# Splitting the first load of a memory-bound decode kernel into 16 and 112 partitions

## Chip, cores, metric

One core of one Trainium2 chip. The metric is the device time of one execution in microseconds (us), the median of several. Times named together were taken in the same rounds on the same chip, unless the text says otherwise.

Names used below: SBUF is the on-chip memory, 128 partitions (rows) wide. PE multiplies matrices, DVE, ACT and POOL are the vector, scalar and general engines; SP issues the transfers. A load is carried out by 16 DMA engines (each load leaves 16 landing records), in packets; here a packet is one row, that is, one partition's share of the load (28672 bytes for `wq`).

## The reference, cut to what matters

```python
# A: attention of one new token over a cache of 65536 positions, 16 query heads, 8 cache heads
xn = layernorm(x)                      # x: (1, 1, 448)
q  = xn @ wq                           # wq: (448, 4096), bf16: 3.67 MB, needed before any score
scores = einsum(q, k_cache) / sqrt(256)  # k_cache: (8, 65536, 256) bf16: 268 MB
o = softmax(scores) @ v_cache          # v_cache: as much again
A = o @ wo
# B: a small gated feed-forward of the same token (w_gate, w_up, w_down)
out = x + A + B
```

Half a gigabyte of cache is read once for one token.

## The kernel before

All large loads are issued from one queue, SP, in the order in which the data are used: `wq`, then blocks of the cache through a ring of four SBUF slots (4 MB each, 128 partitions of 32 KB). The parts that the change and the argument touch:

```python
NSLOT = 4; CH = 64
ring   = S_("ring", [P, NSLOT * SLOT], BF16)     # P = 128, SLOT = 16384 elements
w_area = S_("w_area", [P, WQN], BF16)            # WQN = 14336: 28672 bytes in a partition

def item(key, parts, need=()):                   # one or more loads on the SP queue
    for n in need:
        W("sp", *n)
    for ap, src, sem in parts:
        semtot[sem] = semtot.get(sem, 0) + 16
        items[key] = (sem, semtot[sem])          # who waits for key waits for all its parts
        prog["sp"].append(("d", here[0], ("DMA", key, len(prog["sp"])), (ap, src), sem))

def flat_src(src, n):                            # memory as 128 rows of n elements
    return src.rearrange("a b -> (a b)").rearrange("(p n) -> p n", p=P)

item("wq", [(w_area[:, 0:WQN], flat_src(A_wq, WQN), "wq")])
for u in range(U):
    for c in range(HC):
        slot_item("k", u, c)                     # a ring slot; waits for FREE of 4 rounds ago
# ... [cut: the other loads, all compute, the emitter]
```

PE waits for `wq` (`W_item("pe", "wq")`), makes the queries, and then takes one ring slot after another.

## Time and profile before

| | before |
|---|---|
| time, median of 3 runs | 1284.51 us (1284.49 to 1285.25) |
| span of the profiled run | 1283.4 us |
| PE, DVE, ACT busy | 72%, 46%, 36% |
| bytes on the SP queue | 549.04 MB |
| rate between 60 and 1200 us | 432 GB/s |

The page's slice rows and its queue table. A digit is the busy share of the 16 DMA engines in one fortieth of the span, in tenths; the row below gives the GB/s moved.

```profile
DMA  9999999999999999999999999999999999999997
GB/s 405 427 433 427 433 432 431 430 431 432 432 433 431 433 430 433 430 433 430 433 432 432 432 431 432 429 433 433 431 432 432 432 430 433 431 431 433 431 429 318
...
q1 hardware_dynamic: 22210, 549.04, 99.6%
```

The DMA queue runs from the beginning to the end at one rate. No compute engine comes near that.

The table of issues: the size of one load, and the median time from issue to landing.

```profile
ring<-in_A_k_cache_dram SPq DMA_DIRECT2D x64, 4096.0 KB, 25.0
ring<-in_A_v_cache_dram SPq DMA_DIRECT2D x62, 4096.0 KB, 32.0
...
w_area<-in_A_wq_dram SPq DMA_DIRECT2D x1, 3584.0 KB, 11.3
```

At 432 GB/s, 4 MB take 9.7 us. The cache loads land 25 to 32 us after issue, so each waits behind others: the queue is never empty. Whatever holds the DMA engines up should therefore be added to the end (it was: 7.50 us lost at the start, 7.30 at the end, measured below).

The stretches of the span (us; busy time of each engine; granted clock; DMA busy share; GB/s):

```profile
core 0: us, PE busy (x) PEld busy (x) DVE busy (x) ACT busy (x) POOL busy (x), PEclk, DMA share, GB/s
0.00:10.00 10.00, 0.00 (x0) 0.00 (x0) 4.33 (x12) 1.28 (x1) 4.52 (x35) 1.00 0.85 336
10.00:20.00 10.00, 3.52 (x120) 3.35 (x120) 3.12 (x9) 2.25 (x8) 0.00 (x0) 1.00 1.03 443
20.00:30.00 10.00, 7.13 (x52) 6.51 (x53) 4.12 (x7) 3.22 (x4) 0.00 (x0) 1.00 0.99 426
...
60.00:1200.00 1140.00, 835.79 (x8877) 617.09 (x8876) 537.37 (x998) 421.43 (x596) 0.00 (x0) 0.88 1.00 432
```

The timeline of the start (start, duration, engine, operation; in brackets the idle time before it and what ended that):

```profile
0.74 0.41 SPq L776 DMA_DIRECT2D w_area<-in_A_wq_dram  x1
...
1.21 2.20 SPq L776 DMA_DIRECT2D ring<-in_A_k_cache_dram  x4
...
14.00 3.15 PE L352 MATMUL ps_m<-xnT_sb,w_area 128*128 128x2 bf16 x112 [1.63 <-ACT xnT_sb L340]
...
22.87 5.35 PE L352 MATMUL ps_t<-ident_f,ring 128*128 128x128 f32 x32 [5.72 <-DMA ring<-in_A_k_cache_dram]
```

The issue on SP is over long before its data land (0.41 us against 11.3). The queries wait here for `xnT_sb`, not for `wq`; the first cache block is used as soon as it has landed.

### The profile page before, as it was taken

Reading aid. Unit: us, or ns where it says so; the run is one execution under the profiler, and the core shown is the slowest. Engines: PE = TensorE matmul, PEld = TensorE weight load, DVE = VectorE, ACT = ScalarE, POOL = GpSimd, SP = SyncE. Lnnn points to the kernel's source line nnn. Section 1 sums busy time; section 2 is a strip of 40 time slices with the busy share of each in tenths; the row PEclk is TensorE's granted clock in tenths of the full one; section 3 lists DMA queues with packets and bytes.
Section 4 is the critical chain, followed back from the end, with each engine's and each line's share of the span. In section 5 each row is a group of like instructions: output and inputs, shape, how many; then the busy total and the mean of one; then the engine's idle time right before and its main releaser. Section 6 shows DMA issues by size and latency. Waiting matters only on the chain.

```text
span 1283.4 us, 22878 instructions
## 1 busy us (share of the span) xinstructions
PE 924.9 (72%) x9824; PEld 671.5 (52%) x9824; DVE 585.8 (46%) x1091; ACT 459.2 (36%) x655; POOL 4.5 (0%) x35
## 2 busy tenths in 40 slices
PE   3988766786666886666876667866668766678654
PEld 3867554465454565554654545654446544456411
DVE  4756443554344554444554445543445534455300
ACT  2645332353333443324433243432434333234300
POOL 1000000000000000000000000000000000000000
PEclk9988888998889988879888889888899887898876
DMA  9999999999999999999999999999999999999997
GB/s 405 427 433 427 433 432 431 430 431 432 432 433 431 433 430 433 430 433 430 433 432 432 432 431 432 429 433 433 431 432 432 432 430 433 431 431 433 431 429 318
DMA packets 22228, 549.22 MB, mean 428 GB/s; under 512 B 2371, under 2 KB 4422, under 8 KB 5190
## 3 DMA queue, kind: packets, MB, share of 16 engines
q1 hardware_dynamic: 22210, 549.04, 99.6%
q8 instruction: 8, 0.13, 0.0%
q14 instruction: 6, 0.05, 0.0%
q10 hardware_dynamic: 4, 0.00, 0.0%
HBM read 549.03 MB, written 0.00 MB: 428 GB/s over the span
## 4 chain that ended last, share of the span: by engine, by line
DMA 68%; PE 31%; SPq 0%; ACT 0%; issue 0%; DVE 0%
DMA ring<-in_A_k_cache_dram 63%; PE ps_t L352 24%; PE ps_q L352 5%; DMA w_area<-in_B_w_down_dram 3%; DMA ring<-in_A_v_cache_dram 2%; PE ps_s L352 1%; PE ps_m L352 1%; SPq L776 0%; ACT s L430 0%; DVE res_bf L727 0%; PE ps_o L352 0%
## 5 line engine op out<-in xcount | busy, mean ns | idle before, releaser
L352 PE MATMUL ps_t<-ident_f,ring 128*128 128x128 f32 x4096 | 568.8, 296 | 248.6 <-DMA ring<-in_A_k_cache_dram 229.5
L406 DVE COPY kt_buf<-ps_t 128x1024 bf16<-128x1024 bf16 x768 | 489.5, 683 | 420.9 <-PE ps_t L352 420.4
L352 PEld LDWEIGHTS ps_t<-ident_f,ring 128*128 128x128 f32 x4096 | 494.9, 152 | 354.2 <-DMA ring<-in_A_k_cache_dram 245.5
L408 ACT ACTIVATE kt_buf<-ps_t 128x1024 bf16<-128x1024 bf16 x256 | 261.9, 1023 | 356.1 <-PE ps_t L352 355.8
L430 ACT ACTIVATE s<-ps_q 98x512 bf16<-98x512 f32 x256 | 152.7, 597 | 288.1 <-PE ps_q L352 288.1
L352 PE MATMUL ps_o<-ring,p_sb 128*4 128x512 bf16 x2048 | 132.6, 401 | 67.0 <-DMA ring<-in_A_v_cache_dram 67.0
L352 PE MATMUL ps_q<-kt_buf,q_cur 128*2 128x512 bf16 x2048 | 166.2, 402 | 0.0
L352 PEld LDWEIGHTS ps_o<-ring,p_sb 128*4 128x4 bf16 x2048 | 47.7, 86 | 133.2 <-issue 75.5
L352 PEld LDWEIGHTS ps_s<-sel_bf,s 128*128 128x128 bf16 x1024 | 60.7, 99 | 54.1 <-ACT s L430 50.7
L540 DVE CAST ob_sb<-ps_o 100x512 bf16<-100x512 f32 x29 | 20.0, 691 | 142.8 <-PE ps_o L352 142.8
L352 PE MATMUL ps_s<-sel_bf,s 128*128 128x8 bf16 x1024 | 64.4, 169 | 22.6 <-ACT s L430 22.6
L497 ACT ACTIVATE p_sb<-S_sb 128x128 bf16<-128x128 bf16 x64 | 18.9, 307 | 136.2 <-PE ps_o L352 136.0
L576 DVE TENSOR_TENSOR rowsf<-ps_m,rowsf 1x448 f32<-1x448 f32 x28 | 17.1, 612 | 53.8 <-PE ps_m L352 53.8
L352 PEld LDWEIGHTS ps_q<-kt_buf,q_cur 128*2 128x2 bf16 x2048 | 27.1, 79 | 10.2 <-issue 5.0
L512 DVE RECIPROCAL rs<-ps_m 128x4 f32<-128x4 f32 x29 | 5.3, 182 | 52.8 <-PE ps_m L352 52.8
L352 PE MATMUL ps_m<-wo_cur,oT_sb 128*1 128x448 bf16 x112 | 25.7, 352 | 0.0
L352 PEld LDWEIGHTS ps_m<-rowsum,ones_f 128*128 128x128 f32 x116 | 15.1, 190 | 12.6 <-issue 12.6
L352 PE MATMUL ps_m<-rowsum,ones_f 128*128 128x2 f32 x116 | 17.6, 256 | 0.0
L352 PEld LDWEIGHTS ps_m<-wo_cur,oT_sb 128*1 128x1 bf16 x112 | 9.3, 83 | 13.5
L454 DVE CAST S_sb<-ps_s 128x256 bf16<-128x256 f32 x32 | 12.9, 404 | 4.3 <-PE ps_s L352 4.3
L487 ACT ACTIVATE S_sb<-S_sb,negmax 128x512 bf16<-128x512 bf16 x16 | 13.4, 864 | 3.6 <-DVE negmax L481 3.6
L456 DVE TENSOR_REDUCE m1p<-S_sb 128x2 f32<-128x256 bf16 x32 | 13.5, 421 | 1.1
(79 smaller groups left out, 138.3 us busy)
## 6 DMA issues: line engine op xcount, KB each, us to landing
ring<-in_A_k_cache_dram SPq DMA_DIRECT2D x64, 4096.0 KB, 25.0
ring<-in_A_v_cache_dram SPq DMA_DIRECT2D x62, 4096.0 KB, 32.0
ring<-in_A_v_cache_dram SPq DMA_DIRECT2D x2, 2048.0 KB, 28.1
w_area<-in_A_wq_dram SPq DMA_DIRECT2D x1, 3584.0 KB, 11.3
wo_cur<-in_A_wo_dram SPq DMA_DIRECT2D x7, 448.0 KB, 15.4
ring<-in_A_v_cache_dram SPq DMA_DIRECT2D x2, 1024.0 KB, 30.2
ring<-in_A_v_cache_dram SPq DMA_DIRECT2D x4, 512.0 KB, 31.4
w_area<-in_B_w_gate_dram SPq DMA_DIRECT2D x1, 1568.0 KB, 38.6
```

The source lines that it names most:

```text
L352: return pe.matmul(*a, **k)
L406: O(e, ("EV", s, m), lambda it: nc.vector.tensor_copy(out=kt[:, :], in_=tb[:, :]), f"ev{m}")
L408: O(e, ("EV", s, m), lambda it: nc.scalar.activation(out=kt[:, :], in_=tb[:, :], func=ACTF.Copy), f"ev{m}")
L430: O("act", ("EVQ", s), lambda it: nc.scalar.activation(out=s2[s % 2][0:QROWS, :], in_=ps_q[0:QROWS, :], func=ACTF.Copy), "evq")
L454: O("dve", ("SCOPY", u), lambda it: nc.vector.tensor_copy(out=S, in_=ps_sn))
L456: O("dve", ("SMAX", u), lambda it: nc.vector.tensor_reduce(out=m1p[:, :, k], in_=S.rearrange("p n i -> p i n"), axis=AX.X, op=ALU.max))
L487: O("act", ("EXP", h, i), lambda it, i=i: nc.scalar.activation(out=S_sb[:, :, i], in_=S_sb[:, :, i], func=ACTF.Exp, bias=negmax[:, i:i + 1 ...
L497: O("act", ("PC", t, c), lambda it: nc.scalar.activation(out=p_sb[:, c, :, :], in_=S_sb[:, n:n + CH, :], func=ACTF.Copy), "pc")
L512: O("dve", ("RS", t), lambda it: nc.vector.reciprocal(out=rs[:, :, :], in_=ps_m[0:P, C_TOT:C_TOT + NH * rep]))
L540: O("dve", ("OB", t), lambda it: nc.vector.tensor_copy(out=ob_sb[0:OROWS, :], in_=ps_o[0:OROWS, :]))
L576: O("dve", ("RES", t), lambda it: nc.vector.tensor_tensor(out=base_f, in0=ps_m[0:1, C_BIG:C_BIG + D], in1=base_f, op=ALU.add))
```

## The change

The changed kernel begins with a load of 16 rows, one for each of the 16 DMA engines; the other 112 rows follow. The change states no reason; presumably data were to move sooner.

```diff
-    item("wq", [(w_area[:, 0:WQN], flat_src(A_wq, WQN), "wq")])
+    item("wq", [(w_area[o:e, 0:WQN], flat_src(A_wq, WQN)[o:e, :], "wq") for o, e in ((0, P // 8), (P // 8, P))])
```

## The prediction

> What bounds the kernel now: the DMA queue. The page's slice rows show DMA busy 9 tenths in every slice but the last (7), at about 432 GB/s except the first (405) and the last (318). The issue table shows cache loads landing 25 to 32 us after issue, so work is always queued; the chain of waits is 68% DMA. PE (72%), DVE and ACT wait. The time is: start to first packet, the packets of 16 engines, a tail of some 6 us. The trace's packet records put the first packet at 1.77 us, 1.03 us after the first issue began; that issue occupies SP for 0.41 us (timeline). A 28672-byte packet takes 1.06 us (27.0 GB/s per engine), back to back; those of the first round took 1.4 to 2.3 us.
>
> The change: the order of instructions differs only on SP: the load of wq into 128 partitions becomes 16 and then 112. Bytes and packets stay the same, save 16 semaphore packets of 9 ns. Issues behind it move by some 0.4 us, which doesn't matter: 8 us of wq is queued. Gain: the issue of 16 rows is shorter, so the first packet may start earlier. The issue of 128 rows is 0.41 us, of one row 0.21 us (timeline), so I estimate 0.1 to 0.2 us, all on the critical path.
>
> Cost: every other big load covers 128 partitions. [...] This trace can't confirm it; it shows each engine at 27.0 GB/s when 128 partitions are written. [...] The second part gives seven rows to each engine. [...] Lost DMA time isn't regained, so it goes to the end one for one.
>
> Prediction: 1290 us, range 1284 to 1297. Faster by over 2%: 0.01; within 2%: 0.93; slower by over 2%: 0.06.
>
> What would show it:
> - First packet 0.1 to 0.2 us earlier: the 16-row issue under 0.41 us in the timeline.
> - [...] the first slice falls below 405 GB/s. [...]
> - [...]
> - wq landing (11.3 us after issue) becomes 15 to 19 us; PE's first transposes start 3 to 7 us after the 22.87 us of before; later slices keep 432 GB/s.
> - PE, DVE and ACT busy times unchanged.
>
> What would make it wrong: [...] If rows are dealt by 16, it is near 1310. If the engine that ends last (landings of the last load spread over 3 us) is not the one delayed most, the loss is a microsecond or two smaller.

The sum behind the 1290 us: 1284.4 us with the gain alone (1284.5 less 0.1), and, for the case that came about, two terms for the cost of the two parts, together 2.4 to 7.2 us: 1286.8 to 1291.6 us in all. Both cost terms were estimates. The landing of `wq` and PE's start were forecast with them; so was the 1310 us of the case of dealing by 16.

## The result, and the profile after

| | before | after |
|---|---|---|
| time, median of 4 runs each | 1284.7 us | 1292.35 us |
| range of the runs | 1284.49 to 1285.25 | 1292.07 to 1292.52 |
| ratio of the runs | | 1.0059 (95%: 1.0041 to 1.0076) |
| span of the profiled run | 1283.4 us | 1290.7 us |
| PE busy | 924.9 us | 926.4 us |

A ratio is the mean time of one kernel's runs over that of the other's of the same rounds, so it is not quite the ratio of the medians. The change costs 7.65 us by the medians, 0.6%. The two profiled executions happen to be the slowest of each kernel (1285.25 and 1292.52), so the traces below show 7.3 us and not 7.65.

The page's slice rows and queue table of the changed kernel:

```profile
DMA  9999999999999999999999999999999999999997
GB/s 307 423 434 434 429 432 433 428 437 429 432 434 429 435 431 432 433 431 434 431 432 432 431 434 431 433 432 431 434 430 434 432 430 435 430 434 432 430 431 317
...
q1 hardware_dynamic: 22226, 549.04, 99.6%
```

The same bytes, and 16 packets more. The busy row has not changed by one digit, but the first slice moved 307 GB/s in place of 405. A packet that is held up lasts longer in the records (3.04 us in place of 1.73 in the first round below) and counts as busy for all of it; one has to read the GB/s row as well.

The issues of the changed kernel:

```profile
ring<-in_A_k_cache_dram SPq DMA_DIRECT2D x64, 4096.0 KB, 25.3
ring<-in_A_v_cache_dram SPq DMA_DIRECT2D x62, 4096.0 KB, 32.3
...
w_area<-in_A_wq_dram SPq DMA_DIRECT2D x1, 3136.0 KB, 18.3
...
w_area<-in_A_wq_dram SPq DMA_DIRECT2D x1, 448.0 KB, 5.8
```

The stretches of the changed kernel:

```profile
core 0: us, PE busy (x) PEld busy (x) DVE busy (x) ACT busy (x) POOL busy (x), PEclk, DMA share, GB/s
0.00:10.00 10.00, 0.00 (x0) 0.00 (x0) 5.11 (x15) 2.35 (x3) 4.55 (x35) 1.00 0.91 184
10.00:20.00 10.00, 0.70 (x21) 0.65 (x22) 2.34 (x7) 0.79 (x5) 0.00 (x0) 1.00 0.99 285
20.00:30.00 10.00, 2.79 (x105) 2.70 (x102) 0.00 (x0) 0.40 (x2) 0.00 (x0) 1.00 0.98 421
...
60.00:1200.00 1140.00, 841.42 (x8945) 620.10 (x8943) 542.34 (x1005) 425.33 (x601) 0.00 (x0) 0.88 1.00 432
```

In the first 20 us the DMA engines are as busy as before (0.91 and 0.99) and move 184 and 285 GB/s where they moved 336 and 443. After 60 us the rate is again 432.

The timeline of its start:

```profile
0.74 0.85 SPq L776 DMA_DIRECT2D w_area<-in_A_wq_dram  x2
...
1.64 1.85 SPq L776 DMA_DIRECT2D ring<-in_A_k_cache_dram  x4
...
19.66 3.12 PE L352 MATMUL ps_m<-xnT_sb,w_area 128*128 128x2 bf16 x112 [8.39 <-DMA w_area<-in_A_wq_dram]
...
30.14 5.57 PE L352 MATMUL ps_t<-ident_f,ring 128*128 128x128 f32 x32 [7.36 <-DMA ring<-in_A_k_cache_dram]
```

The queries now wait for `wq`. That wait costs nothing by itself: the next data, the first cache block, land only at 30.10 us. It is a sign of the DMA delay, not a second loss.

The delay is complete when `wq` has landed, and is carried to the end. The trace's landing records, us from the span's start, last of the 16 engines:

| | before | after | difference |
|---|---|---|---|
| first packet starts | 1.77 | 1.76 | -0.01 |
| issue of the first load, duration | 0.41 | 0.39 | -0.02 |
| all of `wq` landed | 12.03 | 19.53 | 7.50 |
| first cache block landed | 22.82 | 30.10 | 7.28 |
| last load landed | 1277.97 | 1285.27 | 7.30 |
| span | 1283.4 | 1290.7 | 7.3 |

The packet records show how. They are the large packets of the SP queue in order of start, taken 16 at a time, since the load has 16 engines; the table gives the median duration of each round in us. Rounds 1 to 8 are `wq`, 28672 bytes a packet; rounds 9 and 10 are the first cache block, 32768 bytes. (Grouped by start, not by engine, so a round can hold a neighbour's packet.)

```
round     1     2     3     4     5     6     7     8     9    10
before  1.73  1.08  1.06  1.06  1.06  1.06  1.06  1.06  1.21  1.21
after   3.04  2.42  1.92  1.60  1.53  1.65  1.90  1.80  1.75  1.21
```

Rounds 1 to 9 add up to 10.39 us before and 17.61 us after: 7.2 us. From round 10 on both are alike.

### The profile page after: what moved, and what is told of

It is laid out like the page before. It is cut to its first block, busy times and chain, and to the rows that moved or that the text cites. A ratio compares the mean times of both kernels' runs of the same rounds, so it can differ in the third digit from the quotient of the medians.

```text
span 1290.7 us, 22879 instructions
## 1 busy us (share of the span) xinstructions
PE 926.4 (72%) x9824; PEld 671.7 (52%) x9824; DVE 586.1 (45%) x1091; ACT 459.5 (36%) x655; POOL 4.6 (0%) x35
## 4 chain that ended last, share of the span: by engine, by line
DMA 68%; PE 31%; SPq 0%; ACT 0%; issue 0%; DVE 0%
DMA ring<-in_A_k_cache_dram 63%; PE ps_t L352 24%; PE ps_q L352 5%; DMA w_area<-in_B_w_down_dram 3%; DMA ring<-in_A_v_cache_dram 2%; PE ps_s L352 1%; PE ps_m L352 1%; SPq L776 0%; ACT s L430 0%; DVE res_bf L727 0%; PE ps_o L352 0%
## 6 DMA issues: line engine op xcount, KB each, us to landing
w_area<-in_A_wq_dram SPq DMA_DIRECT2D x1, 3136.0 KB, 18.3
```

## The experiments

Theories, as the expectations below use them:

- **Ports.** The expectations' name for this: what counts is which SBUF partitions the 16 engines write at the same time. No trace or run here shows a port.
- **Splitting, or cold start.** A second load, or a small load at the very beginning, has a fixed cost.
- **Memory.** Sixteen neighbouring rows read at once are slow on the read side; SBUF doesn't matter.

Medians in us; "over" is the difference of the medians to the kernel before in the same rounds.

| run | the first load | this | before | over |
|---|---|---|---|---|
| e_cols | 1/8 and 7/8 of the columns, 128 rows each | 1285.07 | 1285.05 | 0.02 |
| e_quarter | 16 and 112 rows for a quarter of the columns, then one load | 1286.37 | 1285.05 | 1.32 |
| e_dum16 | 16 rows once more, then one load | 1289.0 | 1285.05 | 3.95 |
| e_dum128 | as many bytes once more into 128 rows, then one load | 1286.02 | 1285.05 | 0.97 |
| e_nn | 8 x 16 rows: near in SBUF, near in memory | 1307.54 | 1285.25 | 22.29 |
| e_fn | 8 x 16 rows: far in SBUF, near in memory | 1294.24 | 1285.25 | 8.99 |
| e_nf | 8 x 16 rows: near in SBUF, far in memory | 1307.64 | 1285.25 | 22.39 |
| e_ff | 8 x 16 rows: far in SBUF, far in memory | 1294.35 | 1285.25 | 9.10 |
| e_rev | 112 rows, then 16 | 1293.9 | 1285.17 | 8.73 |
| e_half | 64 rows, then 64 | 1294.2 | 1285.17 | 9.03 |
| e_seven | 16 rows, then 7 x 16 rows with step 7 | 1292.6 | 1285.12 | 7.48 |
| e_dum112 | 112 rows once more, then one load | 1297.43 | 1285.12 | 12.31 |

All twelve passed the comparison with the reference. e_fn and e_nf put rows of `wq` into wrong partitions: the comparison doesn't notice a wrong `wq` in this problem, so it says little about that part of a kernel. These two are wrong by their construction.

### Is it the splitting? e_cols

```diff
-    item("wq", [(w_area[:, 0:WQN], flat_src(A_wq, WQN), "wq")])
+    item("wq", [(w_area[:, a:b], flat_src(A_wq, WQN)[:, a:b], "wq") for a, b in ((0, WQN // 8), (WQN // 8, WQN))])
```

> The first load is again made as two with the same 1 to 7 split of bytes, but by columns: both parts cover all 128 partitions. Port theory (loss comes from which SBUF partitions are written at once): within 0.5 us of the kernel before (about 1284.7), wq landing near 11.5 us after issue, first packet still at 1.77 us. Splitting theory (a second load at the start costs a fixed amount, whatever its shape): about 1292, as in the changed kernel.

Measured: 1285.07 beside 1285.05, ratio 1.0 (95%: 0.9987 to 1.0014). The issues of e_cols:

```profile
w_area<-in_A_wq_dram SPq DMA_DIRECT2D x1, 3136.0 KB, 10.8
...
w_area<-in_A_wq_dram SPq DMA_DIRECT2D x1, 448.0 KB, 3.9
```

The same two sizes as in the changed kernel, landing 10.8 and 3.9 us after issue in place of 18.3 and 5.8. Making two loads costs nothing; how they are cut does. It gains nothing either: its first packet started at 1.76 us.

### Per byte, or once? e_quarter

```diff
-    item("wq", [(w_area[:, 0:WQN], flat_src(A_wq, WQN), "wq")])
+    item("wq", [(w_area[o:e, a:b], flat_src(A_wq, WQN)[o:e, a:b], "wq") for o, e, a, b in
+                ((0, 16, 0, WQN // 4), (16, P, 0, WQN // 4), (0, P, WQN // 4, WQN))])
```

> The split into 16 and 112 rows is made for the first quarter of the columns only; the other three quarters are one load of 128 partitions. Port theory: the loss is per byte, so a quarter of the changed kernel's 7.65 us: 1.9 us, total about 1286.6 (1286.0 to 1287.2). Splitting or cold-start theory: the whole 7 us or more is lost, total about 1292.

Measured: 1.32 us over, within the stated range, though below 1.9. The ratio, 1.0009 (95%: 0.9995 to 1.0022), leaves open whether there is a loss at all (though the fastest of its runs, 1285.62, is above the slowest before, 1285.32), but not one of more than 2.8 us: a fixed cost of 7 us is refuted.

### The first part by itself: e_dum16 and e_dum128

```diff
 ... [cut: "dum" is added to the list of semaphores]
+    item("dum", [(ring[0:16, 3 * SLOT:3 * SLOT + WQN], flat_src(A_wq, WQN)[0:16, :], "dum")])   # e_dum16
+    item("dum", [(ring[:, 3 * SLOT:3 * SLOT + WQN // 8], flat_src(A_wq, WQN)[:, 0:WQN // 8], "dum")])   # or: e_dum128
     item("wq", [(w_area[:, 0:WQN], flat_src(A_wq, WQN), "wq")])
 ...
-                 [("FREE", r - NSLOT)] if r >= NSLOT and k == 0 else ())
+                 [("FREE", r - NSLOT)] if r >= NSLOT and k == 0 else [("DMA", "dum")] if r == NSLOT - 1 else ())
```

> The first part by itself: before wq's unchanged 128-partition load, 16 rows of wq (459 KB) are read once more into partitions 0 to 15 of ring slot 3, which the fourth cache load overwrites later, after a wait for this load. Port theory: [...] the total is 4.25 us over before (1288.9, 1288.3 to 1289.5), 3.2 us over the next kernel, which reads as many bytes into 128 partitions. If the rows-16 part costs nothing beyond its bytes: 1.06 us over before (1285.8).

> Control to the one before: the same 459 KB read once more, as an eighth of the columns of all 128 partitions. All theories: 459 KB at 16 x 27.0 GB/s is 1.06 us, total 1285.8 (1285.3 to 1286.3), unless the extra load itself costs something (splitting theory: about 7 us more).

Measured: 3.95 and 0.97 us over; the ratios' 95% intervals, 1.0017 to 1.0044 and 0.9994 to 1.0021, do overlap a little, but no run of the one lies within 2.5 us of a run of the other. The same bytes at the same place in the queue cost 2.98 us more when they go to 16 partitions. That is the first part of the change's loss.

### SBUF or memory? e_nn, e_fn, e_nf, e_ff

Eight loads of 16 rows each; only the partitions (first index) and the rows of memory (second) differ.

```diff
-    item("wq", [(w_area[:, 0:WQN], flat_src(A_wq, WQN), "wq")])
+    item("wq", [(w_area[16 * b:16 * b + 16, 0:WQN], flat_src(A_wq, WQN)[16 * b:16 * b + 16, :], "wq") for b in range(8)])   # e_nn
+    item("wq", [(w_area[b:P:8, 0:WQN], flat_src(A_wq, WQN)[16 * b:16 * b + 16, :], "wq") for b in range(8)])   # e_fn
+    item("wq", [(w_area[16 * b:16 * b + 16, 0:WQN], flat_src(A_wq, WQN)[b:P:8, :], "wq") for b in range(8)])   # e_nf
+    item("wq", [(w_area[b:P:8, 0:WQN], flat_src(A_wq, WQN)[b:P:8, :], "wq") for b in range(8)])   # e_ff
```

> wq as eight loads of 16 rows, block b being rows 16b to 16b+15 in memory and partitions 16b to 16b+15 in SBUF. Port theory: [...] about 25 us over before, near 1310. Memory theory (16 engines reading 16 neighbouring rows at once are slow on the read side, SBUF does not matter): about the same. Splitting theory: seven more loads, each with a like cost.

> The same eight loads of the same 16 neighbouring rows of memory, in the same order, but written to partitions b, b+8, b+16 and so on[...]. The result is wrong on purpose (rows of wq land in other partitions). Port theory: [...] about 8.5 us over before, near 1293. Memory theory and splitting theory: as the kernel before it, near 1310.

> Eight loads into 16 neighbouring partitions as in the first of this set, but each reads rows b, b+8, b+16 and so on of memory. The result is wrong on purpose. Port theory: as the first, near 1310, since SBUF is written alike. Memory theory: faster, as the reads lie 229 KB apart.

> Eight loads, rows b, b+8, b+16 and so on of memory into the same partitions; the result is right. Port theory: as the second, about 8.5 us over before, near 1293. Memory theory: as the third, whatever that is. Splitting theory: as all three others.

Measured: 22.29, 8.99, 22.39, 9.10 us over. The stretches of each, between 6 and 18 us, which lies inside all four loads of `wq`. For e_nn:

```profile
6.00:18.00 12.00, 0.37 (x8) 0.28 (x8) 5.45 (x16) 1.85 (x6) 0.00 (x0) 1.00 0.98 115
```

For e_fn:

```profile
6.00:18.00 12.00, 0.37 (x8) 0.28 (x8) 4.47 (x14) 1.85 (x6) 0.00 (x0) 1.00 1.04 217
```

For e_nf:

```profile
6.00:18.00 12.00, 0.37 (x8) 0.28 (x8) 5.46 (x16) 1.85 (x6) 0.00 (x0) 1.00 0.97 117
```

For e_ff:

```profile
6.00:18.00 12.00, 0.37 (x8) 0.28 (x8) 4.81 (x15) 1.85 (x6) 0.00 (x0) 1.00 1.08 225
```

The last two columns are the DMA busy share and the GB/s. Changing the partitions alone nearly doubles the rate (115 to 217, 117 to 225); changing the rows of memory alone moves the rate by 2 and 8 GB/s and the time by 0.1 us. So for loads of 16 rows the read side explains next to nothing, and neither does the number of loads, as all four make eight. In the packet records the middle rounds last 3.90 us in e_nn and 2.20 us in e_fn (3.79 in e_nf and 2.22 in e_ff). So 459 KB (16 packets) went at 117.6 GB/s into 16 neighbouring partitions and at 208.5 GB/s into 16 partitions 8 apart. The ratio is 1.8. e_nn came out some 3 us below its forecast: the rounds lasted 3.90 us, less than the estimate.

### Order, and halves: e_rev and e_half

```diff
-    item("wq", [(w_area[:, 0:WQN], flat_src(A_wq, WQN), "wq")])
+    item("wq", [(w_area[o:e, 0:WQN], flat_src(A_wq, WQN)[o:e, :], "wq") for o, e in ((0, 7 * P // 8), (7 * P // 8, P))])   # e_rev
+    item("wq", [(w_area[o:e, 0:WQN], flat_src(A_wq, WQN)[o:e, :], "wq") for o, e in ((0, P // 2), (P // 2, P))])   # e_half
```

> The same two parts in the other order: rows 0 to 111 first, rows 112 to 127 last. Port theory: about the same loss, 5 to 8 us over before (1290 to 1293)[...]. Cold-start theory (the small load is slow only because it is first): most of the loss is gone, 1285 to 1288.

> Two loads of 64 rows, four rows for each engine. If each engine takes four neighbouring rows, [...] about 8.5 us over before (1293). If rows are dealt out 16 at a time, [...] about 25 us over (1310). [...] Splitting theory: as the changed kernel, 1292, which this run alone cannot tell from 1293[...].

Measured: e_rev 8.73 us over. The cold-start theory is refuted, as the loss is there with the small load last. The forecast of the port theory was a miss in size: it allowed 5 to 8 us, and the loss is above that, and 1.1 us more than in the changed kernel (by runs of other rounds, and the ratio's interval, 1.0053 to 1.0080, overlaps that of the change; the traces agree with it: `wq` landed at 20.96 us, against 19.53). In its packet records the 16 rows, now round 8, take 3.53 us, and round 9, the first of the cache block behind them, 2.36 us. Why this order costs more wasn't tested further.

e_half: 9.03 us over; its rounds 2 to 8 last 2.24 us (one of them 2.07). That is near the 2.20 of e_fn, whose 16 partitions lie 8 apart, and far from the 3.90 of e_nn, so 64 rows dealt out 16 neighbours at a time, as e_nn does by hand, are unlikely. The time is near the 1293 of the case of four neighbouring rows to an engine; why that case should cost this much was the author's estimate. This run puts 9.03 us on two loads of 64 rows, 3.67 MB in all.

### Which rows does an engine take in the load of 112? e_seven and e_dum112

```diff
-    item("wq", [(w_area[:, 0:WQN], flat_src(A_wq, WQN), "wq")])
+    item("wq", [(w_area[0:16, 0:WQN], flat_src(A_wq, WQN)[0:16, :], "wq")] + [
+        (w_area[16 + j:P:7, 0:WQN], flat_src(A_wq, WQN)[16 + j:P:7, :], "wq") for j in range(7)])   # e_seven
```

```diff
+    item("dum", [(ring[16:P, 3 * SLOT:3 * SLOT + WQN], flat_src(A_wq, WQN)[16:P, :], "dum")])   # e_dum112, the wait as in e_dum16
     item("wq", [(w_area[:, 0:WQN], flat_src(A_wq, WQN), "wq")])
```

> Which rows does each engine get in the load of 112? Here the first 16 rows are loaded as in the changed kernel, and the other 112 as seven loads of 16 rows with step 7, [...] what it would do in the one load of 112 if it takes seven neighbouring rows. If it does, the time is that of the changed kernel, 7.65 us over before (1292.8 beside a before of 1285.15, within 0.8 us), and rounds of packets last 1.5 to 2.0 us as there. If rows are dealt out otherwise, the time differs by more than that. Splitting theory was refused by earlier runs; eight loads by themselves should cost nothing.

> The second part by itself: rows 16 to 127 of wq (3.21 MB) are read once more into ring slot 3 before the unchanged 128-partition load of wq. [...] If the two parts of the changed kernel's loss add (2.98 us for the first by the two extra-load runs, so 4.7 for the second), the total is 7.43 + 4.7 = 12.1 us over before, 1297.2 (1296.5 to 1298). [...]

Measured: e_seven 7.48 us over, e_dum112 12.31 us over (four runs). The rounds of packets, median us, as above:

```
round     1     2     3     4     5     6     7     8     9    10
after   3.04  2.42  1.92  1.60  1.53  1.65  1.90  1.80  1.75  1.21
e_seven 3.04  2.33  1.94  1.60  1.43  1.56  1.94  1.81  1.76  1.21
```

Seven loads that lay out by hand what one load of 112 would do, if every engine took seven neighbouring rows (and if in each load of 16 the same engine took the same place, which the author assumed), reproduce its time and its rise and fall from round to round within about 0.1 us. That makes neighbouring rows very likely; another dealing with the same pattern isn't excluded, as the records don't name the engine.

The single packets of the changed kernel agree with it in part. In round 4 two packets took 1.98 us and the other 14 at most 1.73; in round 6 four took 1.92 to 2.10 and the others at most 1.76. So some packets are held up more than others, but those others are held up too (1.48 us or more, in place of 1.06), and elsewhere nothing stands out: in rounds 3 and 7 all 16 took 1.89 us or more, in round 5 all took 1.50 to 1.68. e_seven has the two in its round 4 (1.97 and 1.98, the others at most 1.73), with no clear gap in round 6; e_dum112 has no such gaps. What singles those packets out is not shown. One thing is not tested: no run changes the rows of memory of the load of 112 alone, so for this part a slow read side is unlikely by the four runs above, not excluded.

The load of 112 by itself cost 12.31 us where 16 engines at 27.0 GB/s need 7.43 (the first term of the expectation's sum): 4.9 us more. With 2.98 for the first part that makes 7.9, beside 7.65 measured for the whole change. Within the noise of such differences, the two parts add.

No version tried was faster than the kernel before; the nearest, e_cols, is the same.

## Why the prediction was right, and where it was off

That the number came out so near is in part luck. The terms of the case that came about add up to 1286.8 to 1291.6 us, and the measured 1292.35 lies above that. The stated range, 1284 to 1297, was wider than the terms and held even the case of no cost (1284.4). So the time alone says little for the mechanism; the packet records and the experiments do.

- **DMA-bound from first to last packet, and lost DMA time goes to the end one for one: right.** 7.50 us lost when `wq` had landed, 7.30 at the last landing, 7.3 in the span.
- **Gain of 0.1 to 0.2 us from a shorter issue: wrong.** The issue of 16 rows took 0.39 us, that of 112 rows 0.40, that of 128 rows 0.41. The first packet came at 1.76 in place of 1.77 us. Between one row (0.21) and 128 (0.41) the prediction assumed a line, and there is none. The timeline before held a warning: its other load of one row, of `x`, took 0.52 us to issue. In the experiments the issue of 16 rows 8 apart in SBUF (e_fn, e_ff) took 0.62 us, and of 64 neighbouring rows (e_half) 0.57, with the first packet at 2.14 (or 2.13) and 2.10 us; 16, 112 and 128 neighbouring rows took 0.39 to 0.41, with the first packet at 1.75 to 1.77. The cause wasn't tested.
- **First part: right in size.** 2.98 us in isolation. That it comes from the SBUF side, by partition, is shown by e_nn against e_fn (22.29 and 8.99 us over). The first slice fell, as forecast (307 GB/s, from 405). Round 1 read 2.48 to 3.40 us, and round 2 was long too (2.42). The load's last landing came at 6.54 us, 4.8 us after its first packet; in e_nn, where rounds of its kind follow each other, they settle at 3.90.
- **Second part: mis-sized, and the one that put the prediction 2.35 us low.** It was 4.7 us (7.65 less 2.98), 4.9 in isolation, more than the term allowed, and not so different by engine: `wq` landed on the 16 engines between 18.12 and 19.53 us, before between 11.19 and 12.03. Neighbouring rows, one of the cases counted, are what e_seven fits. That count let some engines run at full pace. The records don't show any such engine: in rounds 4 to 8 the shortest packet took 1.48 us, against 1.06. Why all are slowed stays open.
- **Dealing 16 at a time, near 1310: not what happens for 112 rows**, but the size was about right: e_nn, which does just that, took 1307.54.
- **wq landing 15 to 19 us after issue (18.3) and later slices at 432 GB/s: right.** First transposes 3 to 7 us later: 7.27, just outside.
- **A loss smaller by a microsecond or two, if the last engine is not the most delayed: not seen.** The end moved by 7.30 us, nearly as much as the landing of `wq` (7.50).
- **Busy times unchanged: right.** PE 924.9 and 926.4 us, DVE 585.8 and 586.1, ACT 459.2 and 459.5.

## What to carry to other kernels

Loads into fewer than 128 partitions ran the DMA engines at a fraction of their rate here: 117.6 GB/s for 16 neighbouring partitions, 205 for 64 (459 KB in 2.24 us) and 261 for 112 (3.21 MB in 12.31 us), beside 432. For 16 partitions the runs show that it matters which of them are written at once (3.90 us a round for neighbours, 2.20 for 16 that lie 8 apart); for 112 that the same is behind it is likely, not shown, and why all engines are slowed is open. In a kernel that is bound by its DMA queue, what 3.67 MB loaded in this way lost at the very start was paid in full at the end (7.50 us and 7.30). Split a load by columns, so that each part covers all 128 partitions (0.02 us here), not by rows (7.5 to 22 us). Read the GB/s beside the DMA busy share: a held-up packet counts as busy.
